# Merging two half-steps of a fused convolution and GELU layer into one step with 512-column matmuls

## The chip, the cores and the metric

One core of one Trainium2 chip. The metric is the device time of one execution in microseconds (us), as the median of repeated runs. All runs quoted here were in the fast state. The experiments ran on three chips; the median of the kernel before differs by 0.6 us between them, so a difference of 1 us or less between kernels of different rounds shows little. Lines such as L486 are line numbers of the kernel whose trace is shown; the same piece of code has other numbers in another kernel.

## The reference, cut to what matters

```python
# x (8, 4096, 192), weight (8, 7), w_in (192, 2048), w_out (2048, 192), all float32
w = softmax(weight)                               # 7 taps for each of 8 heads of 24 channels
a = causal_depthwise_convolution(x, w)            # seven positions back, zeros ahead of the start
h = a.reshape(32768, 192) @ w_in                  # "first products" below
g = h * (1.0 / (1.0 + np.exp(-1.702 * h)))
out = g @ w_out                                   # "second products" below
```

Of the kernel before, what the change touches and what calls it, by code (L numbers as in the profile page):

```python
# [15 lines left out]
def kernel(  # L16
# [48 lines left out]
    N_ST = 2 * N_BIG  # L65
# [14 lines left out]
    f_pool = ctx.enter_context(tc.tile_pool(name="f", bufs=2))  # L80
# [6 lines left out]
    xins, xts, fs = {}, {}, {}  # L87
# [29 lines left out]
    g = consts.tile([P, 2, NU, 4, NK // NU, T], F32)  # L117
# [5 lines left out]
    us = [room[0 : NC * Q, 4, i * T : (i + 1) * T] for i in range(4)]  # L123
    osbs = consts.tile([P, 2, 2 * TOK], F32)

    def half(s, b, u):

        if b in (T1, T2):
            return room[:, 2 * (b - T1) + u, :].rearrange("p (f t) -> p f t", t=T)
        return g[:, s % 2, u, b, :, :]  # L130
# [4 lines left out]
    C11, C12, C21, C22, C31, C32, V2, V3, V4, V5, V6, V7, V8 = range(NB)  # L135
    V1 = C31
    crossed = consts.tile([P, NB, T], F32)
# [9 lines left out]
    ]  # L147

# [48 lines left out]
    flat_osb = osbs.rearrange("p i n -> p (i n)")  # L197
    later = [g[:, 1, u, :, :, :].rearrange("p b f t -> p (b f t)") for u in range(NU)]
    at = [(flat_osb, 0), (flat_room, 3 * PIECE), (later[1], 2 * TOK), (later[1], 2 * TOK + 2 * PIECE)]
    assert 5 * PIECE + R <= 4 * 2 * TOK and 2 * TOK + 4 * PIECE <= 4 * NK // NU * T  # L200
    raw = [t[:, i : i + 2 * PIECE].bitcast(U32) for t, i in at]
    diag = later[0][:, 0 : 2 * K * R].rearrange("p (c k q) -> p c k q", c=2, k=K)


    sel = flat_osb[0:H, 2 * PIECE : 2 * PIECE + NC * P].rearrange("i (c q) -> i c q", c=NC)
    ident = flat_osb[:, 2 * PIECE + NC * P :]
# [3 lines left out]
    def scratch(flat):  # L210
        return [flat[:, j * PIECE : (j + 1) * PIECE].bitcast(U32) for j in range(3)]

    tmp = f_pool.tile([P, NB, T], F32, name="f").rearrange("p b t -> p (b t)")
    sets = [
        scratch(tmp),
# [50 lines left out]
    LATE = 3  # L266

    def split_piece(i):

        lo, hi, m, l, e = words(i)  # L270
        ef = e.bitcast(F32)

        vec.tensor_scalar(m, hi, 0xFFFFF, 1 << 20, op0=ALU.bitwise_and, op1=ALU.bitwise_or)
        vec.tensor_scalar(e, hi, 20, 0x7FF, op0=ALU.logical_shift_right, op1=ALU.bitwise_and)
        if i >= LATE:
            vec.tensor_scalar(
                ef, e, float(LOW + 255), float(LOW), op0=ALU.min, op1=ALU.max
            )

    def split_rest(i):  # L280
# [5 lines left out]
        if i >= LATE:  # L286
# [65 lines left out]
    def sums_w_out():  # L352
        a = [w_out_s[:, i, :, :] for i in range(NS)]
        vec.tensor_add(a[S1], a[A21], a[A22])
        vec.tensor_sub(a[S3], a[A11], a[A21])
        vec.tensor_sub(a[S2], a[S1], a[A11])
        vec.tensor_sub(a[S4], a[A12], a[S2])
# [48 lines left out]
    def conv(big, c, k, ns=slice(0, 2)):  # L406
        src = conv_src(big, c, k, ns)
        dst = fs[big][:, 2 * c + ns.start : 2 * c + ns.stop, :]
# [8 lines left out]
    def sums_c(big, i):  # L417
        add_up(lambda j: fs[big][:, j, :], *SUMS_C[i])

    def cross(big, o, b0=0, b1=NB, queue=nc.sync):  # L420
        queue.dma_start(
            out=crossed[halves[1 - o], b0:b1, :], in_=fs[big][halves[o], b0:b1, :]
        )

    def copy_over(big, b):

        act.copy(crossed[halves[1], b, :], fs[big][halves[0], b, :])

    def new_f(big):
        fs[big] = f_pool.tile([P, NB, T], F32, name="f")  # L430


    given, waiting = [0], []

    def cross_even(*what):
        if given[0] < what[0] - 1:
            waiting.append(what)
        else:
            cross(what[0], 0, *what[1:])

    def give(s):
        given[0] = s // 2
        for what in waiting:
            cross(what[0], 0, *what[1:])
        waiting.clear()

    def prepare(big):
# [5 lines left out]
        yield "", 0.0, lambda: new_f(big)  # L453

        for c in (0, 2):
# [3 lines left out]
        yield f"first {big}", 0.0, lambda: cross_even(big, V1, C32 + 1)  # L459
        for k in range(K):  # L460
            yield "", 0.76 if k else 0.48, lambda k=k: conv(big, 1, k)
        yield "", 0.0, lambda: cross_even(big, 0, V1)
        for i in range(1, len(SUMS_C)):
            yield "", 0.38, lambda i=i: sums_c(big, i)
        yield f"all {big}", 0.0, lambda: cross_even(big, C32 + 1, NB)

    def product1(slot, a, b, s, first=False):
        f, o = fs[s // 2], s % 2
        for j in range(2):
            for h in range(2):  # L470

                nc.tensor.matmul(  # L472
                    slot[:, h, j * T : (j + 1) * T],
                    w_in_s[halves[h], a, j * P : (j + 1) * P],
                    (f if h == o else crossed)[halves[h], b, :],
                    start=(first and j == 0),
                    stop=True,
                    skip_group_check=True,
                )

    def terms(s, slot, *ts, first=False):
        for t in ts:
            product1(slot, *TERMS[t], s, first)
            first = False

    def gelu(s, b, u, src):  # L486
        act.activation(  # L487
            half(s, b, u).rearrange("p f t -> p (f t)"),
            src.rearrange("p h n -> p (h n)"),
            AF.Gelu_apprx_sigmoid,  # L490
        )

    def sum_g(s, u, dst, terms):
        vec.tensor_sub(half(s, dst, u), half(s, terms[0], u), half(s, terms[1], u))  # L494

    def sum_1(s, u):
        sum_g(s, u, T1, (B12, B11))

    def sum_2(s, u):
        sum_g(s, u, T2, (B22, T1))  # L500

    def sum_3(s, u):
        sum_g(s, u, T3, (B22, B12))

    def sum_4(s, u):
        sum_g(s, u, T4, (T2, B21))

    def plain(s, u, m, n, slot, ks=range(NC), first=0):

        for k in ks:  # L510
            product1(slot, NC * (2 * u + m) + k, 2 * k + n, s, k == first)

    def hidden(s, x, z, y, sums, work, fetch, last=lambda: None):


        second = s % 2

        def pe(slot, *ts, first=False):
            terms(s, slot, *ts, first=first)


        if second:
            pe(z, 7, first=True)
        pe(sums, 12)
        act.copy(k15, sums)
        pe(x, 5, 17)
        gelu(s, B11, 0, x)
        if not second:
# [4 lines left out]
        work(3.2 if second else 1.5)  # L533
# [10 lines left out]
        gelu(s, B12, 0, sums)  # L544
# [4 lines left out]
        gelu(s, B22, 1, k19)  # L549
        gelu(s, B22, 0, k15)  # L550
# [6 lines left out]
        gelu(s, B11, 1, k20)  # L557
        pe(x, 18)
        gelu(s, B21, 1, x)
        fetch()  # L560
        if not second:

            act.copy(y, z)  # L563
        gelu(s, B21, 0, k16)
        if second:
            sum_1(s - 1, 0)
        else:
            work(1.2)
# [3 lines left out]
        return lambda: gelu(s, B12, 1, k18)  # L572

    def product2(s, slot, bank, ab, last, first=True):

        dst = slot[:, bank, 0:T]
        tiles = [(c, *ab, c) for c in range(NC)] + [(NC, *last)]
        for j in range(NK):
            for l, a, b, c in tiles:
# [3 lines left out]
                    half(s, b, j // (NK // NU))[:, j % (NK // NU), :],  # L583
# [6 lines left out]
    def quarters(s, slot, bank, a, b, c):  # L590

        dst = [slot[l * Q : (l + 1) * Q, bank, 0:T] for l in range(4)]
        for i in range(NK // 4):
            for l in range(4):
                j = NK // 4 * l + i
                nc.tensor.matmul(  # L596
                    dst[l],
                    w_out_s[:, a, j, c * Q : (c + 1) * Q],
                    half(s, b, j // (NK // NU))[:, j % (NK // NU), :],
# [6 lines left out]
    class Out:  # L606


        def __init__(self, s):
            self.s = s  # L610
            self.osb = osbs[0 : NC * Q, s % 2, :].rearrange(
                "q (n j e) -> q n j e", n=2, e=2 * Q
            )

        def turn(self, m, n, src):
            vec.transpose(  # L616
                self.osb[:, n, :, m * Q : (m + 1) * Q],
                src.rearrange("p (j t) -> p j t", t=Q),
            )

        def store(self):
            big, odd = divmod(self.s, 2)
            p, c = divmod(big, CHUNKS)
            t = c * TOK + odd * T
            for n in (1, 0):
                rows = out_v[n, p, t : t + T, :].rearrange(
                    "(j i) (c e) -> c i j e", i=Q, e=2 * Q
                )
                for c in range(NC):

                    (act if c % 2 and self.s == N_ST - 1 else nc.sync).dma_start(
                        out=rows[c], in_=self.osb[c * Q : (c + 1) * Q, n, :, :]
                    )

    def chunk(t, c):
        return t[c * Q : (c + 1) * Q, :]

    def output(s, ra, rb, work, between=None):


        out = Out(s)
        u1, u2, p3, p4 = us

        p1, p3c = product2(s, ra, 0, (A11, B11), (S4, B22, 0))
        act.copy(u1, p1)
        act.copy(chunk(p3, 0), p3c)
        if s % 2 == 0:
            sum_2(s, 0)
        sum_1(s, 1)
        sum_2(s, 1)  # L650
        work(0.7 if s % 2 else 1.5)
        p2, p3c = product2(s, rb, 0, (A12, B21), (S4, B22, 1))
        act.copy(chunk(p3, 1), p3c)
        vec.tensor_add(u2, u1, p2)
        out.turn(0, 0, u2)
        sum_4(s, 0)
        sum_4(s, 1)
        p6, p3c = product2(s, ra, 1, (S2, T2), (S4, B22, 2))
# [255 lines left out]
```

## The kernel before: what the change and the argument touch

The kernel works on pairs of sequences, 512 positions of each at a time: 32 such pairs of steps, numbered by `big`. Both matrix products are made from fewer, recombined block products. The first is done by 21 `terms`, the second by seven products p1 to p7 of a two-by-two scheme. The partial results meet in four accumulators of two banks each (`slots` and `sums`).

The program gives each engine its instructions in a fixed order. VectorE does the convolutions (`conv`), the differences between block products, and the additions at the output; ScalarE does the copies out of the accumulators and the GELU. Preparation of the next pair is a list, `todo`. `work(us)` puts as many of its VectorE operations at that place in the program as fit in the stated time: it is filler for times in which VectorE would otherwise wait.

```python
def product1(slot, a, b, s, first=False):          # L472: one first product, four matmuls of 256 columns
    f, o = fs[s // 2], s % 2
    for j in range(2):
        for h in range(2):
            nc.tensor.matmul(slot[:, h, j * T : (j + 1) * T],
                             w_in_s[halves[h], a, j * P : (j + 1) * P],
                             (f if h == o else crossed)[halves[h], b, :], ...)

def hidden(s, x, z, y, sums, work, fetch, last=...):   # the first products of one half-step
    ...
    pe(y, 6, 14, first=True)
    vec.tensor_sub(x, z, k15)                      # L535: TensorE's ninth term needs it
    ...

def output(s, ra, rb, work, between=None):         # the second products of one half-step
    ...
    p5, p4c = product2(s, rb, 1, (S1, T1), (A22, T4, 0))   # L580, 32 matmuls of 256 columns
    q = quarters(s, rb, 0, A22, T4, 2)                     # L596, 8 matmuls
    act.copy(chunk(p4, 0), p4c)                            # L668
    vec.tensor_add(u1, u2, p5)
    ... (five more additions, one transpose)
    if s % 2:
        work(1.5)                                  # filler ahead of the last product
    else:
        sum_1(s + 1, 0)
        sum_2(s + 1, 0)
    p7, p4c = product2(s, ra, 0, (S3, T3), (A22, T4, 1))
    act.copy(chunk(p4, 1), p4c)                    # L681: the "tail" starts here
    vec.tensor_add(u1, u1, p7)
    vec.tensor_add(u2, u2, p7)
    out.turn(1, 1, u1)                             # L616: a transpose
    vec.tensor_sub(u2, u2, p4)
    out.turn(1, 0, u2)
    out.store()
```

The trace holds two records for each of these matmuls: 64 for the 32 of a `product2`, 16 for `quarters`. In the timeline of the kernel before, two records of first products begin together (both at 27.16 us, each 0.38 us long), and four of second products (512.02 to 512.04 us, the next four from 512.23). A "set" below is the two records (first products) or four (second products) that run at the same time.

Step 0 differs: while it computes, the weights, which come in double precision, are rounded to float32 in eight pieces (four of w_in, four of w_out). Each piece passes from VectorE (`split_piece`) to ScalarE (`split_rest`) and back to VectorE (`join_piece`, `round_piece`). In the kernel before, the preparation of pair 1 joins `todo` only behind the last piece:

```python
def prepare_1():
    round_w_out(3)                                 # the eighth piece
    todo.extend(prepare(1))                        # starts with three transposes of x
    ...
```

## Time and profile before

| | before |
|---|---|
| median time of 6 runs | 2370.11 us (2369.37 to 2370.5) |
| span of the profiled execution | 2368.1 us |
| TensorE busy | 2359.7 us |
| one pair, from the chain of waits in order of time | 72.86 us |

The three runs known when the prediction was made had a median of 2369.61 us. The prediction shows the main lines of this profile and how to read them. Two more rows of the chain that ended last are needed later. Their columns are start in us, duration in us, and what ran:

```profile
63.37 31.22 PE slot L580 x576
140.87 3.59 PE sums L580 x64
```

The first is where step 0 reaches its second products. The second is where pair 1, the first full pair, reaches its own. They are two milestones at which any two of these kernels can be compared.

### The profile page before, as it was taken

What the parts mean: (1) busy time and instruction counts of PE and PEld (TensorE: products, weight loads), DVE (VectorE), ACT (ScalarE), POOL (GpSimd) and SP (SyncE); (2) the same over time, 40 slices, a digit from 0 to 9 for tenths busy, and PEclk for the clock granted to TensorE, in tenths of its full rate; (3) what the DMA queues carried; (4) which work ended last, traced back from release to release, by engine and by line L of the source; (5) the groups of instructions that cost most, each with busy time, mean ns of one, the idle gap of its engine ahead of it and who ended that gap; (6) DMA issues with size and microseconds to landing.
All of it is one profiled execution on the core that took longest, in us unless ns stands there. A gap on an engine that the chain in (4) does not pass through costs nothing.

```text
span 2368.1 us, 71902 instructions
## 1 busy us (share of the span) xinstructions
PE 2359.7 (100%) x32602; PEld 1754.3 (74%) x32602; DVE 2027.2 (86%) x2854; ACT 1048.0 (44%) x1367; POOL 9.1 (0%) x30
## 2 busy tenths in 40 slices
PE   9999999999999999999999999999999999999998
PEld 8677777777777777777777777777777777777776
DVE  8898888888888889888888888888888988888866
ACT  6245543345433455334554334543345533355433
POOL 1000000000000000000000000000000000000000
PEclk9999999999999999999999999999999999999999
DMA  7322333222323123231233322232312323123110
GB/s 172 76 43 49 67 61 62 51 47 55 69 57 65 40 48 69 57 65 38 50 67 61 62 51 48 55 69 55 64 40 48 69 57 67 37 50 67 36 38 15
DMA packets 195824, 135.90 MB, mean 57 GB/s; under 512 B 110752, under 2 KB 186016, under 8 KB 193536
## 3 DMA queue, kind: packets, MB, share of 16 engines
q1 hardware_dynamic: 194912, 131.06, 27.7%
q8 instruction: 255, 4.18, 0.7%
q14 instruction: 49, 0.40, 0.1%
q10 hardware_dynamic: 560, 0.13, 0.0%
q0 software_dynamic: 48, 0.13, 0.0%
HBM read 53.15 MB, written 25.17 MB: 33 GB/s over the span
## 4 chain that ended last, share of the span: by engine, by line
PE 99%; DVE 0%; POOL 0%; DMA 0%; issue 0%; SPq 0%; ACT 0%; POOLq 0%; DVEq 0%; ACTq 0%
PE slot L472 36%; PE slot L580 31%; PE sums L580 15%; PE sums L472 13%; PE slot L596 2%; PE sums L596 1%; PE slot L710 1%; DMA out_dram<-osbs 0%; POOL osbs L246 0%; DVE osbs L616 0%; PE sums L375 0%; PE slot L386 0%; DVE room L673 0%; DVE slot L535 0%; DVE w_in_s L319 0%
## 5 line engine op out<-in xcount | busy, mean ns | idle before, releaser
L472 PE MATMUL slot<-f,w_in_s 64*128 64x256 f32 x3940 | 897.2, 377 | 0.5 <-DVE slot L535 0.5
L472 PE MATMUL slot<-crossed,w_in_s 64*128 64x256 f32 x3940 | 896.8, 377 | 0.0
L472 PEld LDWEIGHTS slot<-f,w_in_s 64*128 64x128 f32 x3940 | 734.8, 187 | 54.2 <-issue 8.6
L580 PE MATMUL slot<-g,w_out_s 128*32 128x256 f32 x9792 | 770.9, 379 | 0.0
L472 PEld LDWEIGHTS slot<-crossed,w_in_s 64*128 64x128 f32 x3940 | 734.8, 187 | 42.4 <-ACT slot L563 0.2
L580 PEld LDWEIGHTS slot<-g,w_out_s 128*32 128x32 f32 x9792 | 420.2, 110 | 184.6 <-issue 7.0
L413 DVE SCALAR_TENSOR_TENSOR f<-xt,cw,f 128x512 f32<-128x512 f32 (+1 forms) x570 | 422.3, 741 | 12.7
L580 PE MATMUL sums<-g,w_out_s 128*32 128x256 f32 x4704 | 381.3, 379 | 0.0
L487 ACT ACTIVATE g<-room 128x1024 f32<-128x1024 f32 x310 | 321.5, 1059 | 100.8 <-DVE room L555 59.6
L472 PE MATMUL sums<-f,w_in_s 64*128 64x256 f32 x1460 | 358.5, 377 | 0.0
L472 PE MATMUL sums<-crossed,w_in_s 64*128 64x256 f32 x1460 | 358.5, 377 | 0.0
L580 PE MATMUL slot<-room,w_out_s 128*32 128x256 f32 x4032 | 301.4, 379 | 0.0
L472 PEld LDWEIGHTS sums<-f,w_in_s 64*128 64x128 f32 x1460 | 272.2, 187 | 18.7 <-issue 4.5
L472 PEld LDWEIGHTS sums<-crossed,w_in_s 64*128 64x128 f32 x1460 | 272.2, 187 | 17.7
L580 PEld LDWEIGHTS sums<-g,w_out_s 128*32 128x32 f32 x4704 | 203.9, 110 | 88.3 <-issue 3.3
L580 PEld LDWEIGHTS slot<-room,w_out_s 128*32 128x32 f32 x4032 | 165.7, 110 | 115.5 <-DVE room L660 0.3
L487 ACT ACTIVATE g<-slot 128x1024 f32<-128x1024 f32 x157 | 159.8, 1018 | 106.3 <-PE slot L472 106.3
L494 DVE TENSOR_TENSOR room<-g,room 128x1024 f32<-128x1024 f32 x126 | 154.1, 1223 | 5.5
L580 PE MATMUL sums<-room,w_out_s 128*32 128x256 f32 x2016 | 152.5, 379 | 0.0
L494 DVE TENSOR_TENSOR room<-g 128x1024 f32<-128x1024 f32 x126 | 150.9, 1197 | 0.0
L494 DVE TENSOR_TENSOR g<-g 128x1024 f32<-128x1024 f32 x126 | 148.0, 1214 | 0.0
L494 DVE TENSOR_TENSOR g<-room,g 128x1024 f32<-128x1024 f32 x126 | 145.7, 1194 | 0.0
(172 smaller groups left out, 1929.2 us busy)
## 6 DMA issues: line engine op xcount, KB each, us to landing
xin<-in_x_dram SPq DMA_DIRECT2D x240, 180.0 KB, 5.0
crossed<-f SPq DMA_DIRECT2D x31, 832.0 KB, 5.9
out_dram<-osbs SPq DMA_DIRECT2D x382, 64.0 KB, 2.8
crossed<-f SPq DMA_DIRECT2D x31, 448.0 KB, 3.8
crossed<-f SPq DMA_DIRECT2D x31, 256.0 KB, 2.9
crossed<-f SPq DMA_DIRECT2D x31, 128.0 KB, 2.2
xin<-in_x_dram SPq DMA_DIRECT2D x16, 160.0 KB, 4.3
g<-in_moe_w_in_dram SPq DMA_DIRECT2D x4, 384.0 KB, 13.0
```

What stands on the lines that cost most here:

```text
L413: vec.scalar_tensor_tensor(out=dst, in0=src, scalar=tap, in1=dst, op0=ALU.mult, op1=ALU.add)
L472: nc.tensor.matmul(slot[:, h, j * T : (j + 1) * T], w_in_s[halves[h], a, j * P : (j + 1) * P], (f if h == o else crossed)[halves[h], b, :] ...
L487: act.activation(half(s, b, u).rearrange("p f t -> p (f t)"), src.rearrange("p h n -> p (h n)"), AF.Gelu_apprx_sigmoid,)
L494: vec.tensor_sub(half(s, dst, u), half(s, terms[0], u), half(s, terms[1], u))
L580: nc.tensor.matmul(dst[l * Q : (l + 1) * Q, :], w_out_s[:, a, j, c * Q : (c + 1) * Q], half(s, b, j // (NK // NU))[:, j % (NK // NU), :], ...
L596: nc.tensor.matmul(dst[l], w_out_s[:, a, j, c * Q : (c + 1) * Q], half(s, b, j // (NK // NU))[:, j % (NK // NU), :], start=(i == 0), stop= ...
L710: nc.tensor.matmul(slots[c][halves[h], 0 if h == o else 1, n * T : (n + 1) * T], diag[halves[o], c - 1, k, :], xts[0][halves[o], c, n, Q - ...
```

## The change

The intent: a pair of half-steps becomes one step. Each matmul then streams 512 columns, so half as many are issued, and whatever a matmul costs beyond its columns is paid half as often. The planes of g are laid out by halves of the hidden units, so that a first product covers one half of the units for all 512 positions, and the second product is done once. In step 0 both halves go through the first products together. The diff, cut to its core:

```diff
-    g = consts.tile([P, 2, NU, 4, NK // NU, T], F32)
+    g = consts.tile([P, 4, NU, 2, 2, TOK], F32)
-    crossed = consts.tile([P, NB, T], F32)
+    conv_t = consts.tile([P, 3, NB, T], F32)
-    LATE = 3                       # pieces 3 to 7: exponent clamped on VectorE
+    CLAMP = (0, 3, 4)              # the others: by two more operations on ScalarE
@@ one first product: two matmuls of 512 columns
-    def product1(slot, a, b, s, first=False):
-        for j in range(2):
-            for h in range(2):
-                nc.tensor.matmul(slot[:, h, j * T : (j + 1) * T], ...)
+    def product1(slot, a, b, big, v, first=False):
+        pair = conv_t[:, big % 2 : big % 2 + 2, place(big, b), :]
+        for h in range(2):
+            src = pair[halves[h], :, :] if h == big % 2 else pair[halves[h], ::-1, :]
+            nc.tensor.matmul(slot[:, h, :], w_in_s[halves[h], a, v * P : (v + 1) * P], src, ...)
@@ output: once a pair, on 512 columns
-        if s % 2:
-            work(1.5)
-        else:
-            sum_1(s + 1, 0)
-            sum_2(s + 1, 0)
+        work(1.5 if small else 4.0)
@@ step 0: x of pair 1 and its preparation come with piece 3, not behind the last piece
-        def prepare_1():
-            round_w_out(3)
-            todo.extend(prepare(1))
+        def piece_3():
+            rounds(3, 4)
+            load_x(1)
+            todo.extend(prepare(1))
+        between = [
+            lambda: rounds(2, 3), piece_3, None, lambda: rounds(4, 5), None, lambda: rounds(5, 6),
+            None, lambda: rounds(6, 7), None, last_piece, None, None,
+        ]
+                    gelu(2 * m + n, u, v, slot)
+                    (between.pop(0) or (lambda: work(1.3)))()
@@ the loop over pairs
-        output(s, y, x, work)
-        output(s + 1, x, y, work)
+        output(big, y, x, work, end=None if more else z)
```

`small` is true only for the half-step that is left of step 0. In the kernel after, the numbers that the traces show stand for: L486 `product1`, L503 `gelu`, L547 the difference that was L535, L590 `product2`, L607 `quarters`, L676 the copy that was L668, L677 the addition of p5, L691 to L695 the tail, L625 the transposes into the output, L423 and L425 convolution taps, L332 and L336 sums of w_in, L408 transposes of x, L286 to L317 the rounding of a piece.

## The prediction

The 13.2 us in its sum are what the matmuls were to save, 0.42 us a pair. That was the author's estimate: in the kernel before, all large matmuls have 256 columns, and no trace at hand showed what a wider one takes.

> **What bounds the kernel now.** I read the page's busy line first, then the chain that ended last, then the groups, and at the end the timelines of VectorE and ScalarE at one seam between two steps.
>
> ```profile
> PE 2359.7 (100%) x32602; PEld 1754.3 (74%) x32602; DVE 2027.2 (86%) x2854; ACT 1048.0 (44%) x1367; POOL 9.1 (0%) x30
> PE 99%; DVE 0%; POOL 0%; DMA 0%; issue 0%; SPq 0%; ACT 0%; POOLq 0%; DVEq 0%; ACTq 0%
> ```
>
> TensorE is busy for the whole span and 99% of the chain is TensorE. The view of waits has only three entries for PE, 2.4 us in all, so busy is not waiting in disguise. Nothing but a shorter stream of matmuls, or a new wait, can move the time. The groups say what the stream is made of:
>
> ```profile
> L472 PE MATMUL slot<-f,w_in_s 64*128 64x256 f32 x3940 | 897.2, 377 | 0.5 <-DVE slot L535 0.5
> L580 PE MATMUL slot<-g,w_out_s 128*32 128x256 f32 x9792 | 770.9, 379 | 0.0
> L494 DVE TENSOR_TENSOR g<-g 128x1024 f32<-128x1024 f32 x126 | 148.0, 1214 | 0.0
> ```
>
> All large matmuls have 256 columns. The 377 ns are latencies and overlap, so the rate has to come from the chain in order of time:
>
> ```profile
> 27.11 7.77 PE slot L472 x72
> 286.58 13.95 PE slot L580 x256
> 505.16 13.95 PE slot L580 x256
> 2347.47 3.45 PE sums L580 x64
> ```
>
> First products (L472) run two at a time, on two halves of the rows: 72 records in 7.77 us are 36 sets of 215.8 ns. Second products (L580, L596) run four at a time, on four strips of columns: 64 records in 3.45 us are 16 sets of 215.6 ns. Either way 256 columns take 215.8 ns. L472 has 10,800 records in its four groups, 5,400 sets; L580 and L596 have 21,552, or 5,388 sets; 10,788 sets x 215.8 ns = 2,328 us of the 2,368. The rows at 286.58 and 505.16 are the same place three pairs of steps apart: a pair takes 218.58 / 3 = 72.86 us, of which 336 sets x 215.83 = 72.52, so some 0.34 us of seams. The 31 pairs are 2,259 us; start, step 0 and the tail are the other 110.
>
> [...] 421 ns at 128x256 and 1,214 at 128x1024 give 1.03 ns a column and 157 ns fixed.
>
> **The change part by part.**
>
> *Matmuls.* The terms, products and columns are the same; each set covers twice the columns. Kept at 256 columns are step 0's second products and half-step output (180 sets) and the last pair's final product, which is cut in two (32 sets). Converted are 5,400 + 5,208 - 32 = 10,576 sets, which become 5,288. [...]
>
> *VectorE and ScalarE.* A pair loses 8 of 16 differences of g (now 2,048 columns) and about 12 small output operations, some 20 x 0.157 = 3 us of VectorE. It is not the bound, so this only buys slack.
>
> *The tail of an output.* This is where time can come back. After the last second product the next step needs the scratch that u1 and u2 occupy, and VectorE must reach the difference of L535 before TensorE's ninth term. The seam before:
>
> ```profile
> 541.67 0.37 ACT L681 COPY room<-slot 32x256 f32<-32x256 f32 x1 [2.30 <-PE slot L580]
> 542.32 0.42 DVE L682 TENSOR_TENSOR room<-room,slot 96x256 f32<-96x256 f32 x1
> 543.77 0.44 DVE L616 STREAM_TRANSPOSE osbs<-room 96x256 f32<-96x256 f32 x1
> 545.54 1.22 DVE L535 TENSOR_TENSOR slot<-slot,room 128x1024 f32<-128x1024 f32 x1
> 546.16 1.01 ACT L531 COPY room<-sums 128x1024 f32<-128x1024 f32 x1 [0.75 <-PE sums L472]
> ```
>
> The product ends near 541.4 and the tail at 544.2; L535 ends at 546.8, and TensorE wants its result after eight terms of 0.863 us, at 548.5: 1.7 us of slack. After the change the copy takes about 0.58 us and the five operations 0.65 each in place of 0.35 to 0.42, so the tail ends at 545.7, two convolution taps (1.5 us) follow, and L535's successor ends at 548.3 where TensorE wants it at 548.4. The slack is gone, though not overdrawn by much. The delay runs on: the next differences come 0.4 to 0.8 us later, and the copy that moves the partial sum for the second half ends about when TensorE asks for it, where before there was 0.3 us to spare. I charge **0.2 us a pair, 6 us** in all.
>
> *The middle of an output* looks safe. A product takes 6.87 us. Counting from the end of the first products, T2 is ready at 8.4 and 12.8 us and is wanted from 13.8; T4 at 18.3, wanted from 20.7; T3 at 26.6, wanted at 29.3. The crossing transfers go out when the first products end and have 36 us; the longest of before took 5.9.
>
> *Step 0.* One of the four convolutions on TensorE (13.49 us for four) goes to VectorE, so TensorE gains 3.4 us; it then waits an estimated 1.7 us for the second half's convolution. It comes to the first full pair 2 us earlier, but VectorE does not: twelve sums of w_in (0.4 us each) and two transposes stand behind the tail, where before there were five and one. I expect 3.5 us of wait there, where before the view shows 0.5. Net **+1 us**.
>
> Sum: 2,369.6 - 13.2 + 6 + 1 = about 2,363; since the 6 us rest on slack of the order of my reading error and may well be nearer 2, I set **2361 us**.
>
> **The rivals.** *A: the floor is all there is.* No new wait; 2,369.6 - 13.2 = 2,356, or 2,353 if step 0 keeps its gain. For it: PE waits for nothing now, and VectorE has fewer instructions. Against: the tail's arithmetic. *B: the longer tail becomes a wait.* Every product's results must now be read at 512 columns before the next pair may overwrite their slots; if the tail is 1 us worse than I think, each of 31 pairs loses 0.8 us and the time is 2,380; 1.6 us worse gives over 2,400. For it: VectorE at 86% with order fixed in the program. Against: before, the same seam cost 0.34 us of which none was a wait. *C: [...] the new moving operand costs something.* A first product now reads two planes, one of them in reversed order, in place of 256 adjacent columns. Then the matmuls save nothing and the time is 2,370 to 2,378. [...] *D: the transfers that cross.* Both halves now share one plane, which is free only when the first products of a pair end; a transfer that started late would stop TensorE at the first term of a pair for some 5 us. The order of the changed program speaks against it: the preparation's last sums stand well before the end of the second half.
>
> **Range and chances.** A and a good step 0 set the low end at 2,351; B in a mild form or C the high end at 2,373. More than 2% faster would be under 2,322, and nothing in the change can take 47 us from a stream of the same columns: 0.02. More than 2% slower is over 2,417, which needs 1.9 us of new wait in every pair: 0.03. Within 2%: 0.95.
>
> **What would show it right or wrong.** Right: sets 429 ns apart in the chain; some 16,000 fewer PE records; PE still above 99% of the chain; a pair near 72.6 us; waits of PE on VectorE's L547, or on ScalarE's copies at L543 and L575, of 0 to 0.3 us a pair; VectorE busy near 1,950 us; a wait of 3 to 4 us at the first full pair. Wrong: sets 431.6 ns apart (C); PE waits above 1 us a pair at the head of a step (B), or on the crossing DMA (D). The prediction fails upwards if the tail's new operations with strided outputs take longer than 0.7 us each.

## The result, and the profile after

The kernel after takes 2389.03 us (median of 6 runs, 2388.49 to 2390.86) against 2370.11 us. The ratio is 1.0082, with a 95% interval of 1.0069 to 1.0095. Ratios here are the mean time of one kernel's fast runs over that of the other's of the same rounds, so not quite the ratio of the medians quoted. It is slower by 0.8%, which is "same" at a threshold of 2%; the predicted range was 2351 to 2373 us.

The busy line and the shares of the chain that ended last, of the kernel after:

```profile
PE 2357.3 (99%) x16794; PEld 889.5 (37%) x16794; DVE 1946.2 (82%) x2182; ACT 1023.3 (43%) x1160; POOL 8.3 (0%) x29
PE 79%; DVE 17%; issue 1%; ACT 1%; DMA 1%; SPq 0%; ACTq 0%; DVEq 0%
```

TensorE's records fell from 32,602 to 16,794 and VectorE's busy time by 81 us, as intended. But the chain is no longer 99% TensorE: 17% of it now runs over VectorE. TensorE's busy time fell by only 2.4 us, so where is the gain? The chain of the kernel after in order of time, at the two milestones and then at the same place two pairs apart:

```profile
72.70 31.22 PE slot L590 x576
155.72 7.00 PE sums L590 x64
169.59 6.87 PE sums L590 x64
228.86 27.60 PE slot L590 x256
374.89 27.60 PE slot L590 x256
```

A second product now has 64 records in 6.87 us. They run four at a time, so 16 sets take 429.4 ns each. Two sets of 256 columns took 431.7 ns. The matmuls do save what was expected. The rest of the arithmetic:

| | before | after | difference |
|---|---|---|---|
| step 0's second products start | 63.37 | 72.70 | +9.3 us |
| from there to pair 1's second products | 77.50 | 83.02 | +5.5 us |
| one pair | 72.86 | 146.03 / 2 = 73.01 | +0.15 us |
| from pair 1's second products to the end of the span | 2227.2 | 2231.6 | +4.4 us |

The three parts give 9.3 + 5.5 + 4.4 = 19.2 us, which is the difference of the spans (2387.3 and 2368.1). So three quarters of the loss is in step 0 and the step up to pair 1; the rest is a pair that should have become shorter. TensorE's waits in the kernel after (total us, times, longest):

```profile
PE slot L486 <- ACT g L503: 8.5, 1, 8.5
PE slot L486 <- DVE slot L547: 8.5, 28, 0.3
PE slot L486 <- DVE w_in_s L332: 3.7, 1, 3.7
...
PE slot L486 <- DVE room L308: 1.0, 1, 1.0
```

Before, there were 2.4 us of waits in all. Four entries are new or grown. The one of 8.5 us and the one at the seams (L547) are read below. The one of 3.7 us is TensorE at the first full pair, waiting for sums of w_in that stand behind the tail of step 0 in VectorE's order; the prediction had put it at 3.5. The one of 1.0 us is the wait for the last convolution of step 0: the view names L308, but ScalarE's copy of that convolution, which the matmuls read, ended at the same time (26.50), and in s0_late and work_short the view names the copy.

**The wait of 8.5 us in step 0.** It is said to be for a GELU. The chain shows what the GELU waited for:

```profile
42.69 7.29 DMA xin<-in_x_dram
...
50.39 1.44 DVE xt L408 x2
...
55.07 0.48 DVE w_out_s L287
...
55.57 0.94 ACT w_out_s L302
...
58.44 0.92 ACT g L503
```

In VectorE's and ScalarE's timelines the same places carry their idle time in brackets. First VectorE, then ScalarE:

```profile
50.39 1.44 DVE L408 STREAM_TRANSPOSE xt<-xin 128x576 f32<-128x576 f32 x2 [9.90 <-DMA xin<-in_x_dram]
```

```profile
55.57 0.94 ACT L302 ACTIVATE w_out_s<-w_out_s,bias 128x768 f32<-128x768 uint32 x1 [11.50 <-DVE w_out_s L287]
```

Read backwards: TensorE needs an accumulator that the GELU (L503) frees; the GELU stands in ScalarE's queue behind three operations of a piece of weights, of which L302 is the first; these need VectorE's half of that piece (L287); and VectorE had two transposes of pair 1's x in front of it, whose data landed only at 49.98. All three engines hang on a load that nothing in step 0 needs.

**The clock after a wait.** The view by windows gives TensorE's busy time, the granted clock, and the share and GB/s of DMA, here around the end of the 8.5 us wait and of the 3.7 us wait:

```profile
59.40:62.00 2.60, 2.60 (x6) 0.50 1.19 210
...
117.63:120.40 2.77, 2.77 (x8) 0.50 0.30 65
...
123.10:127.00 3.90, 3.90 (x21) 1.00 0.10 26
```

After each of the two waits the granted clock was 0.50. The twelve records behind either wait are six sets, 2.58 us at the rate above; they took 5.49 and 5.47 us in the chain. Each of these two waits cost another 2.9 us. Not all of that is the clock: in copy_first (below) the same twelve records, behind a wait of 3.12 us for the same sums, took 2.85, as twelve records did early in the kernel after (from 18.44 us, at a granted clock of 1.00):

```profile
118.82 2.85 PE L486 MATMUL slot<-conv_t,w_in_s 64*128 64x512 f32 x12 [3.12 <-DVE w_in_s L332]
```

So some 2.6 us of the 2.9 came with the low clock.

**The wait at each pair.** The seam between one pair's last product and the next pair, in the chain of the kernel after:

```profile
913.57 1.76 PE slot L607 x16
...
915.35 0.59 ACT osbs L676
...
923.26 0.40 DVE conv_t L423
...
923.69 0.68 DVE room L692
...
928.24 1.24 DVE slot L547
...
929.52 4.56 PE slot L486 x20
```

The last product p7 ended at about 922.0, and ScalarE's copy of it ran from 922.22 to 922.80. VectorE could have begun the tail (L692) then, but it began at 923.69: it was still busy with five convolution taps that `work(4.0)` had put there, the last of them the row at 923.26. Everything behind is late, and TensorE resumes only when L547 is done. VectorE had also begun its additions (L677) late, at 915.97, because ScalarE's copy L676 of p5 ran only once the `quarters` matmuls (L607) behind p5 had ended. The order of VectorE's work is then: additions until 920.2, filler until 923.7, tail.

### The profile page after: what moved, and what is told of

Read it like the earlier page. It is cut to its first block, busy times and chain, and to the rows that moved or that the text cites. A ratio compares the mean times of both kernels' runs of the same rounds, so it can differ in the third digit from the quotient of the medians.

```text
span 2387.3 us, 39095 instructions
## 1 busy us (share of the span) xinstructions
PE 2357.3 (99%) x16794; PEld 889.5 (37%) x16794; DVE 1946.2 (82%) x2182; ACT 1023.3 (43%) x1160; POOL 8.3 (0%) x29
## 4 chain that ended last, share of the span: by engine, by line
PE 79%; DVE 17%; issue 1%; ACT 1%; DMA 1%; SPq 0%; ACTq 0%; DVEq 0%
PE slot L590 28%; PE slot L486 28%; PE sums L486 12%; PE sums L590 9%; DVE conv_t L425 5%; DVE osbs L681 3%; DVE osbs L625 3%; PE slot L607 2%; DVE slot L547 2%; DVE room L677 1%; DVE room L692 1%; DVE osbs L679 1%; DVE room L693 1%; ACT osbs L676 1%; DVE room L695 1%
## 5 line engine op out<-in xcount | busy, mean ns | idle before, releaser
L486 PE MATMUL slot<-conv_t,w_in_s 64*128 64x512 f32 x3740 | 863.3, 595 | 21.8 <-ACT g L503 8.5
L590 PE MATMUL slot<-g,w_out_s 128*32 128x512 f32 (+1 forms) x6800 | 788.6, 571 | 0.0
L486 PEld LDWEIGHTS slot<-conv_t,w_in_s 64*128 64x128 f32 x3740 | 358.1, 188 | 482.9 <-issue 381.2
L425 DVE SCALAR_TENSOR_TENSOR conv_t<-xt,cw,conv_t 128x512 f32<-128x512 f32 (+1 forms) x576 | 423.9, 736 | 11.9
L590 PEld LDWEIGHTS slot<-g,w_out_s 128*32 128x32 f32 x6800 | 240.3, 110 | 457.1 <-issue 438.3
L486 PE MATMUL sums<-conv_t,w_in_s 64*128 64x512 f32 x1660 | 405.1, 591 | 0.0
L503 ACT ACTIVATE g<-room 128x1024 f32<-128x1024 f32 x310 | 321.1, 1058 | 108.4 <-DVE room L567 68.6
L590 PE MATMUL sums<-g,w_out_s 128*32 128x512 f32 (+1 forms) x2304 | 335.0, 587 | 0.0
L506 DVE TENSOR_TENSOR g<-g 128x2048 f32<-128x2048 f32 (+1 forms) x126 | 283.1, 2267 | 4.7 <-PE slot L590 2.4
L486 PEld LDWEIGHTS sums<-conv_t,w_in_s 64*128 64x128 f32 x1660 | 158.5, 187 | 203.4 <-issue 159.6
L503 ACT ACTIVATE g<-slot 128x1024 f32<-128x1024 f32 x167 | 169.4, 1017 | 94.0 <-PE slot L486 94.0
L590 PEld LDWEIGHTS sums<-g,w_out_s 128*32 128x32 f32 x2304 | 93.1, 110 | 152.7 <-issue 146.3
L506 DVE TENSOR_TENSOR room<-g 128x2048 f32<-128x2048 f32 (+1 forms) x65 | 145.8, 2243 | 4.3
L506 DVE TENSOR_TENSOR g<-room,g 128x2048 f32<-128x2048 f32 (+1 forms) x64 | 140.2, 2229 | 0.0
L676 ACT COPY osbs<-slot 32x512 f32<-32x512 f32 (+1 forms) x32 | 18.3, 573 | 251.6 <-PE slot L607 251.6
L590 PE MATMUL slot<-room,w_out_s 128*32 128x512 f32 (+1 forms) x816 | 112.9, 567 | 0.0
L590 PE MATMUL sums<-room,w_out_s 128*32 128x512 f32 x768 | 112.7, 592 | 0.0
L677 DVE TENSOR_TENSOR room<-room,slot 96x512 f32<-96x512 f32 (+1 forms) x32 | 21.6, 675 | 91.2 <-ACT osbs L676 91.2
L547 DVE TENSOR_TENSOR slot<-slot,room 128x1024 f32<-128x1024 f32 x62 | 76.2, 1230 | 12.0 <-ACT g L503 10.2
```

The source lines that it names most:

```text
L425: vec.scalar_tensor_tensor(out=dst, in0=src, scalar=tap, in1=dst, op0=ALU.mult, op1=ALU.add)
L486: nc.tensor.matmul(slot[:, h, :], w_in_s[halves[h], a, v * P : (v + 1) * P], src, start=first, stop=True, skip_group_check=True,)
L503: act.activation(g[:, b, u, v, :, :], src, AF.Gelu_apprx_sigmoid)
L506: vec.tensor_sub(*(half(x, u, cols, small) for x in (dst, a, b)))
L590: nc.tensor.matmul(dst[l * Q : (l + 1) * Q, :], w_out_s[:, a, j, c * Q : (c + 1) * Q], half(b, u, cols, small)[:, v, h, :], start=(first a ...
L676: act.copy(chunk(v4, 0), blocks(p4c))
```

## The experiments

All kernels gave correct results and all runs were fast. The edits are against the kernel after; for both_256, both_clamp, both_clamp_fill and best the cut shows only what is new against the version that the expectation names. "Pair" is half the distance of two like rows of the chain two pairs apart.

| kernel | median us (runs) | ratio to before, 95% | pair us |
|---|---|---|---|
| s0_late | 2380.17 (4) | 1.0043, 1.0028 to 1.0057 | 73.01 |
| work_short | 2375.54 (4) | 1.0022, 1.0007 to 1.0037 | 72.49 |
| copy_first | 2421.56 (4) | 1.0219, 1.0202 to 1.0236 | 74.06 |
| both | 2365.26 (4) | 0.9979, 0.9964 to 0.9994 | 72.49 |
| both_256 | 2376.51 (4) | 1.0028, 1.0013 to 1.0044 | 72.86 |
| work_long | 2435.4 (2) | 1.0276, 1.0257 to 1.0295 | 74.59 |
| both_clamp | 2363.9 (5) | 0.9975, 0.9962 to 0.9987 | 72.49 |
| both_clamp_fill | 2362.79 (5) | 0.9969, 0.9957 to 0.9982 | 72.49 |
| best | 2360.44 (5) | 0.9958, 0.9944 to 0.9972 | 72.48 |

The median of before was 2370.49 us beside the first four, 2369.9 beside the next four, and 2370.17 beside the last.

**s0_late: pair 1's preparation joins the list behind the last piece, as before.**

```diff
     def last_piece():
         rounds(7, 8)
         sums_w_out()
+        todo.extend(prepare(1))
     def piece_3():
         rounds(3, 4)
         load_x(1)
-        todo.extend(prepare(1))
```

> Only the order of step 0 differs: the preparation of pair 1 (three transposes and its taps) enters VectorE's list after the last piece of the weights, not after the fourth. Theory 1 (step 0 lost its time because VectorE's first transposes for pair 1 stood in front of the weights' rounding while their input was still in flight, 9.9 us): the second products of step 0 begin 8 to 12 us earlier than the 72.7 us of the changed kernel, the 8.5 us wait of TensorE on a gelu goes, and the time falls by 7 to 11 us, to 2378-2382. Rival (VectorE has the same work to do in step 0 and is its bound whatever the order): the time stays within 3 us of the changed kernel's 2389 and the wait shows up later, at the first full pair. Pairs stay at 73.0 us under both.

Measured: 2380.17 us, 8.9 us less, and the 8.5 us wait is gone (two of 1.6 and 1.1 us appear further on, where TensorE now arrives earlier); pair 1 reaches its second products at 146.84 in place of 155.72. The pair stays at 73.01 us. The order in step 0 is the cause of that wait; that VectorE has too much to do there, the rival, is out.

**work_short: less filler ahead of the last product.**

```diff
-        work(1.5 if small else 4.0)
+        work(1.5)
```

> Only the filler work in front of the last second product of a full output is cut from 4.0 to 1.5 us; what it held is done in later slots. Theory 1 (the chain of VectorE from the end of the quarters to the tail is what TensorE waits for, the tail starts 0.85 us too late): the pair goes from 73.01 to 72.4-72.6 us, PE's waits on the difference of L547 fall from 8.5 us to under 2, the time falls by 12 to 19 us to 2370-2377. Rival (the excess over 168 sets of 429 ns lies in the matmul stream itself, in seams or weight loads): the pair stays at 72.9 or more. Step 0 stays as it is under both.

Measured: 2375.54 us, 13.5 us less. The pair falls by 0.52 us to 72.49, and the waits on L547 leave the view of TensorE's waits. VectorE's timeline at the same seam:

```profile
918.36 0.68 DVE L692 TENSOR_TENSOR room<-room,sums 96x512 f32<-96x512 f32 x1 [1.15 <-ACT osbs L691]
...
922.91 1.23 DVE L547 TENSOR_TENSOR slot<-slot,room 128x1024 f32<-128x1024 f32 x1
```

With two taps in place of five, VectorE idles for 1.15 us until ScalarE's copy, and the kernel is 13.5 us faster for it: here idle time on VectorE cost nothing, where its lateness had cost 0.52 us a pair. From the start of the tail to L547's start are 4.55 us in both kernels (918.36 to 922.91, and 923.69 to 928.24), so only the start moved. TensorE is recorded busy for 1,899.99 us of the stretch from 400 to 2,300 us, against 1,892.15 in the kernel after. That is 0.30 us a pair of the 0.52 (some 26 pairs). The other 0.22 is hidden in the records around the wait. In the kernel after, TensorE's timeline at this seam has a group of four records from 928.20 that lasts 1.02 us, the wait of 0.30, and the next group at 929.52; without a wait the next group starts 0.86 us after such a group, since it overlaps the end of the last, so the wait costs 0.46 us and not 0.30. The twenty records behind it then take 4.40 us to the start of the next group, in place of 4.29. These 0.16 and 0.11 us are the missing 0.22 to within 0.05, and the five other seams looked at show the same.

**copy_first: the reads of p5 go ahead of the quarters in the program.**

```diff
         p5, p4c = product2(rb, 1, (S1, T1), (A22, T4, 0), **some)
-        q = quarters(rb, 0, A22, T4, 2, **some)
         act.copy(chunk(v4, 0), blocks(p4c))
         vec.tensor_add(v1, v2, p5)
+        q = quarters(rb, 0, A22, T4, 2, **some)
```

> Only the order of emission differs: ScalarE's copy of the corner of p5 and the addition of p5 are written ahead of the quarters' matmuls. Theory 1 (the copy waited for the quarters' last matmul, 1.7 us after the product whose result it reads, because of where it was written): the copy starts some 1.5 us earlier, the chain of additions after it too, and the tail starts with the end of the last product; the pair goes to 72.4-72.6 us as with less filler work. Rival (the wait has another cause, or TensorE now waits for the copy before the quarters): the copy starts at the same time, or a new PE wait appears, and the pair stays at 73.0 or more.

Measured: 2421.56 us, much slower: the expected time was missed, and the rival's new wait is what came. The waits on L547 did vanish, and the copy did start as soon as p5 ended. In this kernel's numbers L675 is the copy and L676 the addition of p5. First its entry among the waits, then the chain:

```profile
PE slot L607 <- DVE room L676: 44.9, 32, 1.4
```

```profile
915.64 6.91 PE slot L590 x64
922.57 0.59 ACT osbs L675
...
923.19 0.69 DVE room L676
...
923.92 1.92 PE slot L607 x16
```

The quarters write bank 0 of the accumulator, p5 stands in bank 1, and still TensorE waits 1.4 us for the readers of p5. With the readers behind the quarters in the program, they waited for the quarters (1.76 us); with the readers ahead, the quarters waited for them (1.4 us). In both orders what came first in the program went first, as if the waits held for the whole accumulator and not for a bank. Whether the chip needs such a wait is not shown: these are waits for semaphores that the program carries. The cause of the late start is confirmed, and this is no remedy. Two accumulators for the two might be one; that was not tried.

**both: s0_late and work_short together.**

> The late preparation of step 0 and the short filler work together. Theory 1: the two gains add, since they lie in different stretches: 2389 less 8 to 11 and less 12 to 19 us, so 2359 to 2369, at or below the kernel before (2370). Rival (work that is pushed out of the output comes back as a wait in the first products, or step 0 is VectorE-bound): above 2372.

Measured: 2365.26 us, 23.8 us under the kernel after; the two gains, 8.9 and 13.5, sum to 22.4. This version is faster than the kernel before (ratio 0.9979, with an interval below 1). The two largest of TensorE's remaining waits:

```profile
PE slot L486 <- DVE w_in_s L332: 3.7, 1, 3.7
PE slot L590 <- DVE room L506: 1.6, 1, 1.6
```

These two and two of 1.1 us each occur once, up to pair 1. In the steady state nothing is waited for.

**both_256: the same program, each matmul of 512 columns split into two of 256.**

```diff
-            nc.tensor.matmul(slot[:, h, :], ..., src, ...)
+        for i in range(2):
+            for h in range(2):
+                nc.tensor.matmul(slot[:, h, i * T : (i + 1) * T], ..., srcs[i], ...)
     # product2 and quarters likewise: for i in range(0, W, T), columns i to i + T
```

Theory 1 is that the lower cost of a wide set, 429.4 ns against two of 215.8, is the whole gain of the wide matmuls.

> On top of the version with both waits repaired, every matmul of 512 columns is split again into two of 256, with the same data layout, order and VectorE work. Theory 1 [...]: 5,288 more sets, 13 us more: 2376-2380 against 2365, the pair 72.9 us against 72.49. Rival (the width gives nothing, the change in this version comes from other parts such as fewer seams or weight loads): within 4 us of 2365.

Measured: 2376.51 us, 11.2 us more than `both`. Layout, order and VectorE's work are the same here, so 11.2 us is what the wide matmuls are worth (the two ran on different chips; against before of their own rounds it is 11.8). The edit also doubles the weight loads, so this run does not part what a matmul costs from what its weight load costs. In the chain, where L596 is this kernel's `product2`, the row shows the size of one product, 128 records or 32 sets of 256 columns:

```profile
160.67 6.91 PE sums L596 x128
```

That is 215.9 ns a set, as in the kernel before. The difference to 6.87 us is small, but the pair has 10.5 such products' worth of sets: 168 sets of 512 columns. Measured between like rows, 0.37 us a pair.

**work_long: more filler still.**

```diff
-        work(1.5 if small else 4.0)
+        work(1.5 if small else 5.5)
```

> The changed kernel as it was, with the filler ahead of the last second product at 5.5 us in place of 4.0, two taps more (1.5 us). Theory 1 (VectorE's chain there is already past the end of the product, so each added us is a us of wait): the pair grows by 1.4 to 1.5 us, to 74.4-74.5, and the time by 43 to 47 us, to about 2433. Rival (there is slack left and the wait has another cause): the pair grows by less than 0.5 us, the time stays under 2405.

Measured: 2435.4 us and a pair of 74.59 us, 1.58 us more for 1.5 us of filler. Half of the pairs have their new wait in this entry, the other half a like one of 14.7 us for another accumulator; both name a copy of ScalarE's behind the late tail:

```profile
PE slot L486 <- ACT room L543: 15.7, 15, 1.1
```

With the slack used up, lateness of VectorE at this place went into the time about one for one. At 4.0 the kernel after was 0.52 us over the edge; at 1.5 it has slack (the 1.15 us for which VectorE idles in work_short).

**both_clamp: pieces 2 and 5 to 7 clamped on VectorE.**

```diff
-    CLAMP = (0, 3, 4)
+    CLAMP = (0, 2, 3, 4, 5, 6, 7)
```

> On top of both repairs, the clamp of the exponent of pieces 2, 5, 6 and 7 goes to VectorE (0.56 us each) in place of two passes on ScalarE (1.9 us each), for which VectorE waits 2.07 us a piece with the transposes gone from there. Theory: VectorE reaches the second products of step 0 some 4 us earlier, TensorE's waits of 1.6 and 1.1 us in step 0 go, that on the sums of w_in (3.7 us) stays: 2361-2363. Rival (VectorE has no idle time to win, only more work): 2365 or more.

Measured: 2363.9 us, 1.4 us less, or 0.8 us less when each is set against before of its own round; a bit short of what was expected, and the rival (no gain) is not out by the time alone. The wait on the w_in sums stayed at 3.7 us and only came earlier. How much of the gain reached the end can be read from TensorE's timeline at the first matmuls behind that wait: first `both`, then `both_clamp`, then `both_clamp_fill`.

```profile
109.05 4.42 PE L486 MATMUL slot<-conv_t,w_in_s 64*128 64x512 f32 x12 [3.69 <-DVE w_in_s L332]
```

```profile
107.13 5.45 PE L486 MATMUL slot<-conv_t,w_in_s 64*128 64x512 f32 x12 [3.69 <-DVE w_in_s L332]
```

```profile
106.70 4.54 PE L486 MATMUL slot<-conv_t,w_in_s 64*128 64x512 f32 x12 [3.69 <-DVE w_in_s L332]
```

The clamp brought TensorE there 1.92 us earlier, but the same twelve records then took 1.03 us longer; the mean granted clock from 63 to 120 us was 0.94 in place of 0.97. Pair 1's second products start at 145.20 in place of 146.09, 0.89 us earlier: 1.92 less 1.03. The wait is the same 3.69 us in all three; the time of the twelve records behind it is not (4.42, 5.45 and 4.54 us).

**both_clamp_fill: more filler in step 0, ahead of its second products.**

```diff
-        work(6.5)
+        work(9.0)
```

> As the one before, and the filler at the head of step 0's second products is 9.0 in place of 6.5 us, so that more of the sums of w_in are done before the tail of step 0's output. Theory: the wait on them at the first full pair, 3.7 us, shrinks by about 2 us as long as no earlier wait comes back: 2359-2362, 0 to 2.5 us under the one before. Rival: the work pushed forward delays the turning of the first results and TensorE waits there; no gain or up to 2 us more.

Measured: 2362.79 us, 1.1 us less, just above the expected 2359 to 2362, and not for the expected reason. The wait on the w_in sums did not shrink. By the rows above, TensorE came there 0.43 us earlier: a wait of 1.10 us on L506 in step 0's output had gone, but the first products had run 0.87 us later since the start (27.16 against 26.29). Another 0.91 us came from the twelve records behind the wait (4.54 us in place of 5.45, with a mean granted clock from 63 to 120 us of 0.97 in place of 0.94), which nothing in the edit aims at. A gain of 1.1 us between two such kernels is thus not evidence for the edit.

**best: filler where VectorE waits in the half-step of step 0.**

```diff
         sum_3(1, cols, False)
-        work(0.7)
+        work(2.4 if small else 0.7)
```

> On top of the version with the clamps and the longer first filler, the filler ahead of the quarters in step 0's output is 2.4 in place of 0.7 us, so that four more of the sums of w_in come before the chain that the quarters end, where VectorE still stood idle for 1.8 us. Theory: TensorE's wait of 3.7 us for the sums of w_in at the first full pair falls to 1 us or less, since the sum that its second term reads is then done before the tail; 2359-2361 against 2362.8. Rival (the sums only change places and the wait moves to a later term or to the copies behind the tail): no gain, 2362-2364. The pair stays at 72.49 us.

Measured: 2360.44 us (2358.97 to 2361.88), ratio 0.9958 to before. The time is in the expected range. The wait did shrink, though less than expected:

```profile
PE slot L486 <- DVE w_in_s L332: 2.3, 1, 2.3
```

Pair 1 reaches its second products at 141.95, 1.1 us later than in the kernel before, and the 30 pairs behind win 0.38 us each. TensorE leaves that wait 1.91 us earlier than in both_clamp_fill; 1.34 of it is the shorter wait, and 0.57 was there at the first products already (26.59 against 27.16). This is the fastest version of the study: 9.7 us under the kernel before, 28.6 us under the kernel after. That it lands beside the predicted 2361 us is chance: it is another program, with five edits.

## Why the prediction was wrong

It named 2361 us and the kernel took 2389.03. Its steps, one by one:

**Matmuls, "13.2 us": right in mechanism, close in size.** The set was put at 429 ns and measured 429.4. The pair without waits was to save 0.42 us and saved 0.37 (72.86 to 72.49), and both_256 puts the whole at 11.2 us. That part of a set's cost comes per set and not per column was the author's estimate, which the kernel before, with one width, could not show. The two kernels together show it, with the weight loads counted in: one set of 512 columns took 2.3 ns less than two of 256 (429.4 against 431.7). Rival C, that the matmuls save nothing, is out.

**VectorE: right.** 1946.2 us busy against about 1950, and longer operands bought slack on an engine that was not the bound: a difference of g over 2,048 columns took 2.28 us, where two over 1,024 had taken 2.43.

**The tail, "the tail ends at 545.7": this step failed.** The durations were right: the copy took 0.58 us as estimated, the tail's operations 0.58 to 0.71 in the chain against 0.65. What failed is the start. The working let the tail begin at the end of the product, with VectorE free. It did not add up the filler `work(4.0)` that the diff puts ahead of the tail, nor when VectorE gets to it: only after ScalarE's copy of p5, which is ordered behind the quarters, whose length doubles to 1.76 us. The view of waits of the kernel before has that very dependency:

```profile
ACT room L668 <- PE slot L596: 164.4, 42, 4.0
```

At 256 columns it did no harm. So the tail began 0.9 us after the copy had ended, and the 0.2 us charged for a pair became 0.52. Nothing was left of the 0.37 us won in a pair. Rival B, a longer tail that becomes a wait, had the right kind (0.8 us a pair, where 0.52 was measured), for a reason that was not the one found: the tail was not longer than thought, it was late.

**Step 0, "Net +1 us": this step failed most.** It lost 14.9 us. Its parts: the 3.4 us gain on TensorE is about right (the waits and the low clock of the first stretch add up to 8.55 + 2.91 + 0.98 = 12.4 us, the loss was 9.3, which leaves 3.1). The wait for the convolution was put at 1.7 and was 1.0; the wait at the first full pair was put at 3.5 and was 3.7. That last agreement is partly luck. The prediction counted in that TensorE would come there 2 us earlier; but the wait is 3.69 us in the kernel after, in s0_late, in work_short and in both alike, whenever TensorE came. It hangs on the sums that stand behind the tail, which starts with TensorE's own last product. Two terms were missing from the sum. First, the 8.5 us wait: the order of step 0's program was read for what each engine does, but not for what VectorE's transposes wait for when they move ahead of the rounding. s0_late shows the cause. Second, the clock: the kernel after shows a granted clock of 0.50 behind the waits of 8.5 and 3.7 us, and the fastest version one of 0.66 and then 0.58 behind 2.35 us (see below). The prediction foresaw a wait of 3.5 us and did not add the 2.9 us that follow it. The kernel before did not show them: TensorE's longest wait there was 1.4 us, and the granted clock 1.00 in every stretch read up to 120 us.

**The middle of an output and rival D: right as far as TensorE's waits go.** None of the differences T2 to T4, and no crossing transfer, is among them.

**The sum of the errors.** A pair was predicted at 0.22 us less than before and took 0.15 us more: 30 pairs make 11 us. Step 0 was predicted at +1 and lost 14.9 us: 14 us. Rounding the sum of 2363.4 us down to 2361 makes 2.4, and the base moved by 0.5 us between the two medians of before. That is the 28 us.

**The observables.** "PE still above 99% of the chain" did not hold (79%), nor did "a pair near 72.6 us" (73.01). But the waits on L547, 0.30 us in each of 28 pairs, lie within the 0 to 0.3 us that the prediction had named as right, and below the 1 us that was to be the mark of B. As a test of B the observable was too coarse: the 0.52 us that a pair lost is more than its gain of 0.37. The sets, the records, VectorE's busy time and the wait at the first full pair came as named.

One point stays open: what the low clock costs. By the timelines, the twelve records behind the equal waits of 3.69 us took 4.39 us in s0_late and 5.47 us in the kernel after, and behind 8.69 us in work_short only 4.28. The granted clock behind the wait was 0.82 and then 0.50 in s0_late, and 0.50 and then 0.53 in the kernel after; in work_short it was not read there. Behind 2.35 us in the fastest version they took 4.54, at 0.66 and then 0.58, and behind 3.12 us in copy_first 2.85. So the length of the wait alone does not decide it. What else does was not shown.

## What to carry to other kernels

When a unit of work doubles, every amount of filler that was tuned to the unit has to be worked out again at the place where its engine is next needed: here filler that ran 0.9 us past the end of the product used up a gain on all pairs, and 1.15 us of idle time on the second engine was the cheaper choice. Two transposes moved forward in VectorE's order took their wait of 9.90 us with them, and ScalarE (11.50 us idle) and TensorE (8.5 us) stood behind it; before moving an operation, ask when its data lands. And a wait of TensorE of several us may have to be charged twice, once for itself and once for what follows: behind all but one of the waits of 2.3 us and more for GELUs or sums of w_in that were read in these runs, the next twelve records (24 of half the width in both_256) took 4.28 to 5.49 us in place of 2.85, so 1.4 to 2.6 us longer. Where the granted clock was read there, it was 0.50 to 0.82.
